# GpSimd waits for the end of short VectorE chains: 42 semaphore waits in an unchanged order (attention with mixture of experts, one Trainium2 core)

## The chip, the cores and the metric

The kernel runs on one core of one Trainium2 chip. The metric is the device time of one launch in microseconds (us), a median over runs. The engines are named as the profile names them: PE is TensorE (PEld its weight loads), DVE is VectorE, ACT is ScalarE, POOL is GpSimd, and SP is SyncE, whose queue issues the DMAs.

## What is computed

Attention over pooled keys, and a top-1 mixture of experts on its output, here cut to the lines that matter:

```
# q [4, 12288, 128], kv [4, 384, 32, 128], w_sr [128, 128]; 8 experts, w1 [8,128,1024], w2 [8,1024,128]
kv_pool = kv.reshape(4, 96, 4, 8, 4, 128).mean(axis=(2, 4))      # 768 keys for each batch
k = v = kv_pool.reshape(4, 768, 128) @ w_sr
a = softmax(q @ k.T / sqrt(128))
x = (a @ v).reshape(49152, 128)
logits = x @ w_gate
e = argmax(logits); gate = softmax(logits)[e]                     # for each token
out = gate * (relu(x @ w1[e]) @ w2[e])
```

## The kernel before

The tokens go through in 96 blocks of 512 (24 for each of the four batches). For a block, PE makes the scores of 768 keys in three pairs of 128 x 512 tiles (`s`), ACT takes the exponential of a pair (`e`, line 974), DVE turns scores and exponentials into the weights `r` (line 976), and PE multiplies them with the values (`po`). A pair of scores keeps its place in PSUM until DVE has written `r`, and there are two such places. ACT, DVE and POOL copy the result and split it into two half-precision parts (`xp`, lines 1010 to 1016), a transposing DMA turns it (`x`), and later PE, ACT and POOL do the expert: hidden units (`b<-x,w1U`), the rectifier on ACT (`g`, and `X` for the first third, which POOL splits in lines 1047 and 1049), the way back on PE (`b<-w2U,g`), DVE's multiplication with the gate (`y`, line 1080) and the store. POOL also splits each block of queries (`qp`, lines 955 and 957) and adds up rows of `kv` for the next batch's keys (lines 443 to 455).

Between the blocks stand pieces that occur once for a batch. `keys` makes the 768 keys and their units; `expert` guesses the batch's commonest expert, loads its weights and sorts its hidden units; `marks` and `count_steps` (lines 1420 to 1424) count the tokens for which the guess does not hold; `general_step` (lines 1213 to 1418) does up to 128 of these in full, once after each of the first three batches. In these pieces DVE has chains of short instructions on tiles of 1 to 384 columns, each needing the one ahead of it: `relative` (lines 584 to 588: five instructions on 128 x 8), `count_steps` (four on 128 x 64), `find` and `find2` (seven and ten, lines 1240 to 1258, nearly all on 128 x 1), and others.

What sets the order: every piece of work is an `op` of a `Plan`, with its engine, a planned duration, a planned time and what it needs. `Plan.order` builds a timetable from these and from hand-set shifts (`NUDGE`), and `Plan.issue` writes the instructions out in that order, so that each engine's instruction stream is fixed. An engine runs its stream in order and waits, by semaphores, for the data and buffers that an instruction needs. `lock=True` keeps an op from being planned at the same time as any POOL op or other locked op; it is a rule of the timetable alone, and nothing holds the engines to it when the program runs. At the start of the program PE also multiplies a constant tile (`slots`) as filler, a fixed number of times.

```
o.lock, o.at0 = lock or eng == "POOL", at        # line 133
if o.lock: start = max(start, locked)            # lines 173, 174
```

Of the kernel before, what the change touches and what calls it, by code (L numbers as in the profile page):

```python
# [18 lines left out]
POOL = 4  # L19
# [92 lines left out]
class Op:  # L112
    pass


class Plan:


    all_ways = False
    LAT = {"PE": 0.28, "ACT": 0.14, "DVE": 0.12, "POOL": 0.14, "SP": 0.1}  # L120

    def __init__(self, slots):
        self.ops, self.slots, self.filler, self.filler_start, self.filler_end = [], slots, None, 0.0, 0.0

    def op(self, eng, us, fn, at, needs=(), gives=(), bufs=(), lands=0.0, moves=0.0, lock=False, way=None):


        if way and WAYS.get(way[0], 0) != way[1] and not self.all_ways:
            return
        o = Op()  # L130
        o.way = way
        o.eng, o.us, o.fn, o.at, o.needs, o.gives, o.bufs, o.lands, o.moves = eng, us, fn, at, needs, gives, bufs, lands, moves
        o.lock, o.at0 = lock or eng == "POOL", at
        o.at = at + sum(NUDGE.get(k, 0.0) for k in self.keys(o))
        o.n = len(self.ops)
        for b in bufs:
            b.left += 1
        self.ops.append(o)
# [89 lines left out]

    def issue(self):
        for o in self.order():  # L230
            for b, first in o.slot_of:
                if first:
                    b.tile = b.make(f"{b.pool}{b.slot}")
            o.fn()


@with_exitstack
def attention_moe(ctx: ExitStack, tc, q, kv, w_sr, w_gate, w1, w2, out):
# [23 lines left out]
    for b in range(B):  # L262
        t = b * NB
# [43 lines left out]
    left, steps, steps_i = keep("left", [P, NL]), keep("steps", [P, NL]), keep("steps_i", [P, NL], I32)  # L307
# [7 lines left out]
    own = keep("own", [P, UH + OWN])  # L315
# [51 lines left out]
    PSUM = {"s": 2, "po": 1, "b": 2}  # L367
    plan = Plan({**SBUF, **PSUM})
    op = plan.op

# [4 lines left out]
    def bank():  # L375
        return buf("b", [P, 512])
# [26 lines left out]
    def keys(b, when):  # L403
# [6 lines left out]
        for d in range(NK // D):  # L410
            at, follow = when(d)
# [9 lines left out]
            if b == 0:  # L421
                pt = pair()
                for i in range(0, POOL, 2):
# [6 lines left out]
                    def add(raw=raw, i=i, pt=pt):  # L430
# [5 lines left out]
                       lock=True)  # L436
# [41 lines left out]
        dg = buf("u", [P, P], BF16)  # L478
# [22 lines left out]
        op("DVE", .3, mean, at - 1, [("vTd", b, d) for d in range(KT // 2)], [("mean", b)])  # L501
        op("DVE", .75, unit_own, at, [("mom", b)], [("own", b)], [dg], lock=True)
        op("PE", .1, lambda: mm(pd.tile[:, :P], ones_b, dg.tile, True, True), at + 1, [("own", b)], [("pd", b)],
# [5 lines left out]
        for n, (lo, hi, w) in enumerate(cuts):  # L509
# [53 lines left out]
    def expert(b, at):  # L563
# [6 lines left out]
        cg = buf("cg", [P, 4, E])  # L570
# [61 lines left out]
        sg = buf("sg", [P, 12, NF])  # L632
# [5 lines left out]
        pz, pu = bank(), bank()  # L638
# [39 lines left out]

        op("DVE", .8, near, at + 11.5, [("u2", b), ("mir", b)], [("key", b)], [pu, sg], lock=True)

# [23 lines left out]
        op("DVE", .17, lambda: chosen(0), at + 15, [("less", b, 0)], [("some0", b)], [la, sg])  # L704
        op("DVE", .35, largest, at + 16, [("less", b, 1), ("some0", b)], [("some", b)], [la, sg])
        pb = bank()
# [6 lines left out]
        cl = buf("cl", [P, NC + 1, NF], BF16)  # L713
# [9 lines left out]

        op("DVE", 1.35, classes, at + 18, [("pb", b)], [("class", b)], [la, pb, cl, sg], lock=True)
        pn = bank()
# [32 lines left out]
        ws = buf("ws", [P, 32])  # L758
# [31 lines left out]
        w2e, w2l = buf("w2e", [P, NF, P + 2], F16), buf("w2l", [P, NF, P], F16)  # L790
# [29 lines left out]

        op("DVE", .4, bias, at + 20, [("ws", b)], [("zp", b)], [w2e, sg], lock=True)

# [78 lines left out]

        op("DVE", .35, biases, at + 30, [("pW", b)], [("zb", b)], [pW, zb])
# [17 lines left out]
        op("DVE", .5, constant, at + 26, [("pown", b), ("uy", b)], [("own2", b)], [po_, ow, ws])  # L920
        op("DVE", .6, constant2, at + 31, [("own2", b), ("w2Ug", b), ("w2x", b)], [("w2U", b)], [ow, w2U], lock=True)
        op("DVE", .1, lambda: nc.vector.memset(cn[:, 31:32], 0.0), at + 36,
# [8 lines left out]
    START, LEN = 42.0, 6.8  # L931
# [281 lines left out]
    def general_step(n=None, at=0.0, follow=()):  # L1213
# [3 lines left out]

        def part(eng, us, fn, needs, gives, bufs=(), lands=0.0):
            if n is None:
                for b in bufs:  # L1220
                    if b.tile is None:
                        i = used[b.pool] = used.get(b.pool, -1) + 1
                        b.tile = b.make(f"{b.pool}{i % plan.slots[b.pool]}")
                fn()
            else:
                here = lambda x: ("general", n, x)
                op(eng, us, fn, at + len(used) * 1.6, [*map(here, needs), *(follow if not needs else ())], [here(gives)], bufs,
                   lands)
                used[len(used)] = 0
# [29 lines left out]

        part("DVE", 1.6, find, [], "find", [gs, gi, le])  # L1260
        vT = buf("gk", [P, NK])
# [9 lines left out]

        part("SP", 3.2, load, ["find"], "load", [gi, vT, *raw], 4.5)
        part("DVE", 1.6, find2, ["find"], "find2", [gs, gi, le])


        NT = NJ + 4
        gp = buf("gp", [P, 2 * NT + 2 * P + 4 + C])
# [13 lines left out]

        part("DVE", 2.0, search, ["find2"], "search", [gs, gp])
        pb = tiny([P, 512])
# [9 lines left out]

        part("DVE", 1.5, select, ["pb"], "select", [gs, gp, pb])
        pr = tiny([P, 512])
# [42 lines left out]
        def top():  # L1348
# [6 lines left out]
                                                      bias=nmax(), scale=scale, accum_out=sums()), ["top"], "a", [gs, ps, a])  # L1355
# [36 lines left out]

        part("DVE", .7, weight, ["ex"], "w", [gs])

# [12 lines left out]
        py, o = tiny([P, 512]), buf("pool", [P, C])  # L1407
# [34 lines left out]
    for t in range(NBLK):  # L1442
        block(t)
        if t == NBLK - LAST:
            marks(B - 1, START + (t + 3) * LEN, (B - 1) * NB, t, False)
        if t % NB == NB - 1:
            b = t // NB
            if b < B - 1:
                marks(b, START + (t + 4) * LEN, b * NB, t + 1, True)
            else:  # L1450
                marks(b, START + (t + 3) * LEN, t + 1 - LAST, t + 1, True)
            op("DVE", 1.8, count_steps, START + (t + 5) * LEN + 3, [("left", b)], [("steps", b)])
            if b in STEPS_AFTER:
                general_step(b, START + (t + 10) * LEN, [("steps", b), ("stored", b)] + [("o", i) for i in range(b * NB, t + 1)])
# [39 lines left out]
```

## Time and profile before

| | us |
|---|---|
| median of 3 runs | 817.34 (816.2 to 818.12) |
| profiled execution | 819.5 |
| its span, from the first to the last instruction | 817.7 |

| engine | busy us | share of the span |
|---|---|---|
| PE | 759.8 | 93% |
| DVE | 652.2 | 80% |
| POOL | 601.1 | 74% |
| ACT | 592.2 | 72% |

The chain of work that ended last lies 62% on PE, 18% on DVE, 7% in DMAs, 6% on POOL and 3% on ACT. PE had its full clock in nearly all of the span. To read it: the shares are averages over 96 nearly equal blocks and a few places that differ from them, so the stretches are looked at one by one.

### The profile page before, as it was taken

Reading aid. Unit: us, or ns where it says so; the run is one execution under the profiler, and the core shown is the slowest. Engines: PE = TensorE matmul, PEld = TensorE weight load, DVE = VectorE, ACT = ScalarE, POOL = GpSimd, SP = SyncE. Lnnn points to the kernel's source line nnn. Section 1 sums busy time; section 2 is a strip of 40 time slices with the busy share of each in tenths; the row PEclk is TensorE's granted clock in tenths of the full one; section 3 lists DMA queues with packets and bytes.
Section 4 is the critical chain, followed back from the end, with each engine's and each line's share of the span. In section 5 each row is a group of like instructions: output and inputs, shape, how many; then the busy total and the mean of one; then the engine's idle time right before and its main releaser. Section 6 shows DMA issues by size and latency. Waiting matters only on the chain.

```text
span 817.7 us, 21949 instructions
## 1 busy us (share of the span) xinstructions
PE 759.8 (93%) x8535; PEld 597.3 (73%) x8535; DVE 652.2 (80%) x1224; ACT 592.2 (72%) x949; POOL 601.1 (74%) x802
## 2 busy tenths in 40 slices
PE   5978999999998988999998978999999999999996
PEld 4547777788786766788776756787787777787875
DVE  5767876888877988878979888788896899868684
ACT  1435878778788766877878767888878878788773
POOL 0543599976779978996778788987767888566545
PEclk9989999999999999999999999999999999999999
DMA  9642999894589987897659789979467789757543
GB/s 338 207 99 53 185 210 256 185 208 103 111 212 173 240 201 190 201 172 169 118 138 218 161 208 222 233 166 202 109 127 153 162 165 226 147 116 136 126 84 93
DMA packets 328282, 139.45 MB, mean 171 GB/s; under 512 B 214590, under 2 KB 320194, under 8 KB 328176
## 3 DMA queue, kind: packets, MB, share of 16 engines
q1 hardware_dynamic: 327696, 137.80, 76.4%
q8 instruction: 67, 1.10, 0.6%
q14 instruction: 39, 0.32, 0.1%
q0 software_dynamic: 192, 0.17, 0.1%
q10 hardware_dynamic: 288, 0.07, 0.0%
HBM read 59.12 MB, written 26.94 MB: 105 GB/s over the span
## 4 chain that ended last, share of the span: by engine, by line
PE 62%; DVE 18%; DMA 7%; POOL 6%; issue 3%; ACT 3%; SPq 0%; DVEq 0%; POOLq 0%; ACTq 0%
PE b L353 30%; PE po L353 17%; PE s L353 13%; DVE r L976 8%; DMA qT<-qp 4%; DMA kv<-in_kv_dram 2%; POOL kv L443 2%; DVE y L1080 1%; ACT e L974 1%; DVE junk L1181 1%; DVE xp L1011 1%; POOL g L1049 1%; DMA x<-xp 1%; DVE la L698 1%; DVE PU L746 0%
## 5 line engine op out<-in xcount | busy, mean ns | idle before, releaser
L976 DVE SCALAR_TENSOR_TENSOR r<-s,e 128x1024 bf16<-128x1024 f32 x288 | 346.2, 1215 | 66.5 <-ACT e L974 64.7
L974 ACT ACTIVATE e<-s 128x1024 f32<-128x1024 f32 x288 | 292.5, 1026 | 95.8 <-PE s L353 88.1
L353 PE MATMUL po<-v,r 128*128 128x145 f16 x2304 | 253.7, 228 | 6.7 <-DVE xp L1011 3.2
L353 PE MATMUL s<-qT,KT 128*128 128x512 f16 x576 | 170.5, 384 | 20.1 <-DVE r L976 12.7
L353 PEld LDWEIGHTS <-r 128*128 128x128 bf16 x2304 | 169.1, 99 | 26.9 <-DVE xp L1011 3.8
L353 PE MATMUL b<-w2U,g 128*128 128x128 f16 x1736 | 159.8, 219 | 1.0 <-POOL g L1049 1.0
L353 PE MATMUL b<-x,w1U 128*128 128x512 f16 x465 | 141.9, 381 | 4.2 <-ACT g L1053 1.4
L353 PE MATMUL po<-M,qT 128*128 128x136 f16 x1152 | 131.8, 224 | 0.0
L353 PE MATMUL b<-L,x 128*128 128x128 f16 x1116 | 123.0, 219 | 0.6 <-ACT pT L467 0.3
L1053 ACT ACTIVATE g<-b,zb 128x512 f16<-128x512 f32 x146 | 99.4, 689 | 25.8 <-PE b L353 24.9
L1049 POOL TENSOR_TENSOR g<-X,g 128x512 f16<-128x512 f32 x96 | 112.8, 1175 | 6.5
L957 POOL TENSOR_TENSOR qp<-qr,qp 128x512 f16<-128x512 f32 x94 | 110.4, 1175 | 5.3
L353 PEld LDWEIGHTS <-g 128*128 128x128 f16 x1736 | 113.0, 98 | 1.2 <-POOL g L1049 1.1
L353 PEld LDWEIGHTS <-qT 128*128 128x128 f16 x1152 | 85.4, 98 | 32.2 <-issue 6.9
L353 PEld LDWEIGHTS <-x 128*128 128x128 f16 x1116 | 81.0, 98 | 17.8 <-issue 2.8
L1047 POOL CAST g<-X 128x512 f16<-128x512 f32 x96 | 60.8, 634 | 41.5 <-ACT X L1045 37.5
L353 PEld LDWEIGHTS <-KT 128*128 128x128 bf16 x576 | 51.2, 100 | 53.4 <-issue 23.2
L955 POOL CAST qp<-qr 128x512 f16<-128x512 f32 x94 | 59.1, 630 | 36.7 <-DMA qr<-in_q_dram 25.2
L1080 DVE TENSOR_TENSOR y<-b,gt 128x512 f32<-128x512 f32 x96 | 65.3, 681 | 17.8 <-PE b L353 12.7
L1045 ACT ACTIVATE X<-b,zb 128x512 f32<-128x512 f32 x96 | 66.4, 693 | 16.8 <-PE b L353 16.1
L353 PEld LDWEIGHTS <-w1U 128*128 128x128 f16 x480 | 45.6, 99 | 35.5 <-issue 4.3
L443 POOL TENSOR_TENSOR kv<-kv,kv 128x1024 f32<-128x1024 f32 x27 | 63.6, 2356 | 6.3 <-DMA kv<-in_kv_dram 5.4
(365 smaller groups left out, 992.3 us busy)
## 6 DMA issues: line engine op xcount, KB each, us to landing
qr<-in_q_dram SPq DMA_DIRECT2D x96, 256.0 KB, 3.4
out_dram<-y SPq DMA_DIRECT2D x96, 256.0 KB, 2.8
kv<-in_kv_dram SPq DMA_DIRECT2D x41, 512.0 KB, 6.5
raw<-in_moe_w_dram SPq DMA_DIRECT2D x14, 512.0 KB, 5.5
e<-in_kv_dram SPq DMA_DIRECT2D x3, 512.0 KB, 8.6
v_dram<-vT SPq DMA_DIRECT2D x4, 384.0 KB, 2.9
qT<-qp SPq DMA_TRANSPOSE x94, 3.4
x<-xp SPq DMA_TRANSPOSE x93, 3.5
```

Source lines behind the costliest of these rows:

```text
L353: return nc.tensor.matmul(o, l, r, start=start, stop=stop)
L443: nc.gpsimd.tensor_add(flat(to), flat(to), flat(of))
L698: nc.vector.tensor_scalar(lc(2 + NC * j, NC), limits, lc(j), key(j), op0=ALU.is_ge, op1=ALU.mult)
L955: op("POOL", .62, lambda: nc.gpsimd.tensor_copy(qp.tile[:, 0], qr.tile), T - 1.9 * LEN, [("qr", t)], [("qh", t)], [qr, qp])
L957: op("POOL", 1.17, lambda: nc.gpsimd.tensor_sub(qp.tile[:, 1], qr.tile, qp.tile[:, 0]), T - 1.8 * LEN, [("qh", t)], [("qp", t)], [qr, qp])
L974: op("ACT", 1.03, lambda e=e, ps=ps: nc.scalar.activation(e.tile, ps.tile, AF.Exp), at + .6, [("s", t, s)], [("e", t, s)], [ps, e])
L976: op("DVE", 1.22, lambda e=e, ps=ps, s=s: nc.vector.scalar_tensor_tensor(r.tile[:, 2 * s:2 * s + 2], ps.tile, 1.0, e.tile, op0=ALU.add, op ...
L1045: op("ACT", .69, lambda ph=ph, zu=zu: nc.scalar.activation(gf.tile, ph.tile, AF.Relu, bias=zu()), at + .5, [("ph", t, u), ("zb", b)], [("g ...
L1047: op("POOL", .62, lambda: nc.gpsimd.tensor_copy(gg.tile[:, 0], gf.tile), at + 1.5, [("gf", t)], [("gh", t), ("g", t)], [gf, gg])
L1049: op("POOL", 1.16, lambda: nc.gpsimd.tensor_sub(gg.tile[:, UH], gf.tile, gg.tile[:, 0]), at + 2, [("gf", t), ("gh", t)], [("g", t)], [gf, gg])
L1053: op("ACT", .69, lambda u=u, ph=ph, zu=zu: nc.scalar.activation(gg.tile[:, u], ph.tile, AF.Relu, bias=zu()), at + .5, [("ph", t, u), ("zb" ...
L1080: op("DVE", .69, lambda: nc.vector.tensor_tensor(y.tile, py.tile.rearrange("p (c d) -> p c d", d=C), bc(gr["gt"].tile[:, 0, js], C), op=AL ...
```

## The change

POOL's stream and all others keep their order. Fourteen kinds of DVE op get the mark `whole=True`. When such an op has been written out, the next POOL op in the order, if the timetable starts it within 2.5 us after the marked op's planned end, gets a semaphore wait on the marked op's last instruction. There are 42 such places, each wait on one instruction, and one POOL op at most for each marked op. In 19 of them POOL's instruction already had a wait, and a separate waiting instruction stands ahead of it.

```diff
 class Op:
-    pass
+    whole = False
 class Plan:
+    FOLLOW = 2.5
-        o.lock, o.at0 = lock or eng == "POOL", at
+        o.lock, o.at0, o.whole = lock or eng == "POOL", at, whole
     def issue(self):
+        block, last = self.tc.nc.cur_bb.bb, None
         for o in self.order():
             for b, first in o.slot_of:
                 if first:
                     b.tile = b.make(f"{b.pool}{b.slot}")
+            n = len(block.instructions)
             o.fn()
+            if o.whole:
+                last = o, block.instructions[-1]
+            if o.eng == "POOL" and last and o.start < last[0].start + last[0].us + self.FOLLOW:
+                first = next(i for i in block.instructions[n:] if i.engine == mybir.EngineType.Pool)
+                self.tc.add_manual_dep(first, last[1].name, mybir.DependencyInfo(
+                    mybir.DependencyClass.Sync, mybir.DependencyReason.DATA), reason="order")
+                last = None
...
-        op("DVE", 1.0, relative, at + 2, [("first", b)], [("cg", b)], [cg], lock=True)
+        op("DVE", 1.0, relative, at + 2, [("first", b)], [("cg", b)], [cg], lock=True, whole=True)
...
-            op("DVE", 1.8, count_steps, START + (t + 5) * LEN + 3, [("left", b)], [("steps", b)])
+            op("DVE", 1.8, count_steps, START + (t + 5) * LEN + 3, [("left", b)], [("steps", b)], whole=True)
```

The other twelve marks are set in the same way: in `keys` on `unit_own`; in `expert` on `near`, `largest`, `classes`, `bias`, `biases` and `constant2`; in `general_step` on `find`, `find2`, `search`, `select` and `weight`.

## Rows read from the trace of the kernel before

**Rows 1.** The page, part 1: busy time, share of the span and instructions by engine.
```profile
PE 759.8 (93%) x8535; PEld 597.3 (73%) x8535; DVE 652.2 (80%) x1224; ACT 592.2 (72%) x949; POOL 601.1 (74%) x802
```
**Rows 2.** Waits of PE: who waited for whom, us in total, times, longest.
```profile
PE s L353 <- DVE r L976: 12.7, 19, 5.7
```
**Rows 3.** Timeline, 38.9 to 58: start, us, instruction, [idle before, releaser].
```profile
38.96 4.78 POOL L443 TENSOR_TENSOR kv<-kv,kv 128x1024 f32<-128x1024 f32 x2
39.57 1.76 DVE L584 TENSOR_SCALAR cg<-iota_e,con 128x8 f32<-128x8 f32 x1
...
41.57 2.19 DVE L586 TENSOR_TENSOR cg<-cg,wg_raw 128x8 f32<-128x8 f32 x1
...
43.87 2.33 POOL L443 TENSOR_TENSOR kv<-kv,kv 128x1024 f32<-128x1024 f32 x1
43.99 2.24 DVE L588 TENSOR_SCALAR cg<-wg_raw,cg 128x8 f32<-128x8 f32 x1
...
47.41 0.59 PE L353 MATMUL s<-qT,KT 128*128 128x512 f16 x1 [5.65 <-DVE r L976]
...
57.60 0.20 POOL L665 TENSOR_TENSOR sg<-sg 128x8 f32<-128x8 f32 x1 [9.25 <-DVE sg L658]
```
**Rows 4.** Lines 584, 586, 588: ns minimum/median/maximum, first and last start us.
```profile
L584 DVE TENSOR_SCALAR cg<-iota_e,con x4: 218/460/1764, 39.6 to 562.0; 128x8 f32<-128x8 f32 x4
...
L586 DVE TENSOR_TENSOR cg<-cg,wg_raw x4: 166/589/2195, 41.6 to 562.9; 128x8 f32<-128x8 f32 x4
...
L588 DVE TENSOR_SCALAR cg<-wg_raw,cg x4: 231/526/2239, 44.0 to 563.3; 128x8 f32<-128x8 f32 x4
```
**Rows 5.** Stretches: us, PE, PEld, DVE, ACT, POOL busy (count), PE clock, DMA share, GB/s.
```profile
47.40:53.20 5.80, 5.79 (x17) 2.54 (x17) 3.54 (x3) 2.05 (x2) 0.87 (x2) 0.50 0.27 68
...
292.10:295.50 3.40, 3.40 (x12) 1.24 (x10) 3.19 (x19) 1.81 (x3) 0.40 (x2) 0.50 0.28 80
...
479.80:483.20 3.40, 3.40 (x28) 2.85 (x26) 1.88 (x3) 1.37 (x3) 2.36 (x4) 0.50 0.67 157
```
**Rows 6.** Timeline, 286 to 292: the first `count_steps` on DVE, and PE behind it.
```profile
286.47 2.23 DVE L1422 TENSOR_SCALAR steps_i<-steps_i 128x64 int32<-128x64 int32 x1
...
288.74 1.31 DVE L1423 CAST steps<-steps_i 128x64 f32<-128x64 int32 x1
...
291.87 0.30 PE L353 MATMUL po<-v,r 128*128 128x145 f16 x2 [1.97 <-DVE r L976]
```
**Rows 7.** Lines 1422 to 1424: ns minimum/median/maximum over the four batches.
```profile
L1422 DVE TENSOR_SCALAR steps_i<-steps_i x4: 195/615/2230, 286.5 to 812.8; 128x64 int32<-128x64 int32 x4
...
L1423 DVE CAST steps<-steps_i x4: 195/618/1309, 288.7 to 813.1; 128x64 f32<-128x64 int32 x4
...
L1424 DVE TENSOR_TENSOR_SCAN ends<-steps x4: 291/678/2359, 290.1 to 813.3; 128x64 f32<-128x64 f32 x4
```
**Rows 8.** Timeline, 474 to 481: the second `count_steps`, PE and POOL behind it.
```profile
474.70 1.04 DVE L1423 CAST steps<-steps_i 128x64 f32<-128x64 int32 x1
...
475.77 2.36 DVE L1424 TENSOR_TENSOR_SCAN ends<-steps 128x64 f32<-128x64 f32 x1
...
478.76 0.22 PE L353 MATMUL po<-v,r 128*128 128x145 f16 x1 [2.89 <-DVE xp L1011]
...
480.68 0.22 POOL L1114 TENSOR_TENSOR gt<-gt 128x16 f32<-128x16 f32 x1 [2.70 <-DVE gt L1111]
```
**Rows 9.** Timeline, 489 to 499: `find2` on DVE, `g` on POOL, its first reader on PE.
```profile
489.42 0.61 POOL L1047 CAST g<-X 128x512 f16<-128x512 f32 x1
...
491.52 0.45 DVE L1255 TENSOR_TENSOR gs<-gs 128x1 f32<-128x1 f32 x1
...
492.25 0.27 DVE L1258 TENSOR_TENSOR step<-step,gs 128x1 f32<-128x1 f32 x1
...
495.67 1.69 POOL L1049 TENSOR_TENSOR g<-X,g 128x512 f16<-128x512 f32 x1
...
498.89 0.39 PE L353 MATMUL b<-w2U,g 128*128 128x128 f16 x4
```

More of the change, by code (lines that the diff above doesn't have):

```diff
@@ L123, in __init__, with op @@
         self.ops, self.slots, self.filler, self.filler_start, self.filler_end = [], slots, None, 0.0, 0.0
-    def op(self, eng, us, fn, at, needs=(), gives=(), bufs=(), lands=0.0, moves=0.0, lock=False, way=None):
+    def op(self, eng, us, fn, at, needs=(), gives=(), bufs=(), lands=0.0, moves=0.0, lock=False, way=None,
+           whole=False):
         if way and WAYS.get(way[0], 0) != way[1] and not self.all_ways:
@@ L368, in attention_moe @@
     plan = Plan({**SBUF, **PSUM})
+    plan.tc = tc
     op = plan.op
@@ L501, in keys @@
         op("DVE", .3, mean, at - 1, [("vTd", b, d) for d in range(KT // 2)], [("mean", b)])
-        op("DVE", .75, unit_own, at, [("mom", b)], [("own", b)], [dg], lock=True)
+        op("DVE", .75, unit_own, at, [("mom", b)], [("own", b)], [dg], lock=True, whole=True)
         op("PE", .1, lambda: mm(pd.tile[:, :P], ones_b, dg.tile, True, True), at + 1, [("own", b)], [("pd", b)],
@@ L677, in near @@
                                            op1=ALU.bitwise_or)
-        op("DVE", .8, near, at + 11.5, [("u2", b), ("mir", b)], [("key", b)], [pu, sg], lock=True)
+        op("DVE", .8, near, at + 11.5, [("u2", b), ("mir", b)], [("key", b)], [pu, sg], lock=True, whole=True)
         def spread():
@@ L704, in expert @@
         op("DVE", .17, lambda: chosen(0), at + 15, [("less", b, 0)], [("some0", b)], [la, sg])
-        op("DVE", .35, largest, at + 16, [("less", b, 1), ("some0", b)], [("some", b)], [la, sg])
+        op("DVE", .35, largest, at + 16, [("less", b, 1), ("some0", b)], [("some", b)], [la, sg], whole=True)
         pb = bank()
@@ L722, in classes @@
             nc.vector.scalar_tensor_tensor(c[:, 2], col(7), top(2), c[:, NC], op0=ALU.is_lt, op1=ALU.subtract)
-        op("DVE", 1.35, classes, at + 18, [("pb", b)], [("class", b)], [la, pb, cl, sg], lock=True)
+        op("DVE", 1.35, classes, at + 18, [("pb", b)], [("class", b)], [la, pb, cl, sg], lock=True, whole=True)
         pn = bank()
@@ L819, in bias @@
             nc.vector.tensor_tensor(z[:, :, P + 1], col(5), z[:, :, P], op=ALU.subtract)
-        op("DVE", .4, bias, at + 20, [("ws", b)], [("zp", b)], [w2e, sg], lock=True)
+        op("DVE", .4, bias, at + 20, [("ws", b)], [("zp", b)], [w2e, sg], lock=True, whole=True)
         pL = bank()
@@ L900, in biases @@
             nc.vector.scalar_tensor_tensor(zb.tile, zb.tile, 1.0 / Z_DOWN, own[:, :UH], op0=ALU.mult, op1=ALU.add)
-        op("DVE", .35, biases, at + 30, [("pW", b)], [("zb", b)], [pW, zb])
+        op("DVE", .35, biases, at + 30, [("pW", b)], [("zb", b)], [pW, zb], whole=True)
         op("ACT", .7, lambda: nc.scalar.activation(w2U.tile[:, :UH], wide()[:, :, :P],
@@ L920, in expert @@
         op("DVE", .5, constant, at + 26, [("pown", b), ("uy", b)], [("own2", b)], [po_, ow, ws])
-        op("DVE", .6, constant2, at + 31, [("own2", b), ("w2Ug", b), ("w2x", b)], [("w2U", b)], [ow, w2U], lock=True)
+        op("DVE", .6, constant2, at + 31, [("own2", b), ("w2Ug", b), ("w2x", b)], [("w2U", b)], [ow, w2U], lock=True, whole=True)
         op("DVE", .1, lambda: nc.vector.memset(cn[:, 31:32], 0.0), at + 36,
@@ L1216, in general_step, with part @@
         used = {}
-        def part(eng, us, fn, needs, gives, bufs=(), lands=0.0):
+        def part(eng, us, fn, needs, gives, bufs=(), lands=0.0, whole=False):
             if n is None:
@@ L1227, in part @@
                 op(eng, us, fn, at + len(used) * 1.6, [*map(here, needs), *(follow if not needs else ())], [here(gives)], bufs,
-                   lands)
+                   lands, whole=whole)
                 used[len(used)] = 0
@@ L1258, in find2 @@
             nc.vector.tensor_tensor(step, step, u(7), op=ALU.add)
-        part("DVE", 1.6, find, [], "find", [gs, gi, le])
+        part("DVE", 1.6, find, [], "find", [gs, gi, le], whole=True)
         vT = buf("gk", [P, NK])
@@ L1272, in general_step @@
         part("SP", 3.2, load, ["find"], "load", [gi, vT, *raw], 4.5)
-        part("DVE", 1.6, find2, ["find"], "find2", [gs, gi, le])
+        part("DVE", 1.6, find2, ["find"], "find2", [gs, gi, le], whole=True)
         NT = NJ + 4
@@ L1290, in search @@
             nc.vector.memset(q_sb(), 0.0)
-        part("DVE", 2.0, search, ["find2"], "search", [gs, gp])
+        part("DVE", 2.0, search, ["find2"], "search", [gs, gp], whole=True)
         pb = tiny([P, 512])
@@ L1302, in select @@
             nc.vector.tensor_tensor(sel0(), sel(), sel0(), op=ALU.subtract)
-        part("DVE", 1.5, select, ["pb"], "select", [gs, gp, pb])
+        part("DVE", 1.5, select, ["pb"], "select", [gs, gp, pb], whole=True)
         pr = tiny([P, 512])
@@ L1391, in weight @@
             nc.vector.tensor_tensor(z(3), z(0), z(2), op=ALU.mult)
-        part("DVE", .7, weight, ["ex"], "w", [gs])
+        part("DVE", .7, weight, ["ex"], "w", [gs], whole=True)
         h = buf("gp", [P, NF, TAIL])
```

## The prediction

> **What bounds the kernel now.** First the busy table of the page: PE is busy for 759.8 of 817.7 us, DVE for 652.2, POOL for 601.1 [rows 1]. So PE sets the time, and an edit that touches only DVE and POOL can win no more than PE's idle time and what PE loses at half clock. Next the waits of PE: it stands 12.7 us before the scores `s`, waiting for DVE's `r`; one of the 19 waits is 5.7 us long [rows 2]. The timeline shows what DVE does in that wait: three instructions on 128 x 8 take 1.76, 2.19 and 2.24 us [rows 3], while the same lines take 0.22, 0.17 and 0.23 at best [rows 4]. Their ends are those of POOL's additions of `kv`: POOL's pair runs from 38.96 to 43.74 and DVE's second long one ends at 43.76; POOL's third runs from 43.87 to 46.20 and DVE's third ends at 46.23 [rows 3]. The short instruction is held until POOL's long one is over, and `r`, queued behind it on DVE, is held too. The same is seen in `count_steps` at 286 [rows 6] and at 474 [rows 8]. Last the PE clock: after each of these three waits PE stays at 0.50, the lower of its two levels (1.2 GHz instead of 2.4), and is busy all the time [rows 5].
>
> **The change, part by part.** No instruction moves and nothing is added on DVE, PE, ACT or SP. On POOL 42 instructions wait for the end of a DVE chain, so that a chain which has not met a POOL instruction yet meets none. The gain is the stretching of the chain; the price is that POOL, and everything queued behind its waiting instruction, starts later. Of the added waiting instructions the trace of before shows nothing that I can price apart; they stand in POOL's idle time before the wait ends, and I count them at zero (bounds: none, and the 1.0 us of the last term).
>
> *The start (38.9 to 53).* Stretching: (1.76 - 0.22) + (2.19 - 0.17) + (2.24 - 0.23) = 5.57 us [rows 3, 4]. The waiting POOL instruction is the very one at 38.96, so the chain, which begins at 39.57, runs clean and ends near 40.66; `r` comes 5.6 us earlier and of PE's 5.65 us some 0.1 is left: -5.5. POOL begins 1.7 us later, and the 9.25 us in which it sits idle before 57.60 [rows 3] hide that; without this cover the 1.7 us would fall on the first `mirror` and on PE behind it. With the idle time goes the cause of the half clock that stands right behind it: 5.79 us of PE work at 0.50 would take 2.9 us at full clock [rows 5]. That is -2.9 if PE alone sets the pace and 0 if the clock falls all the same; I take -2.2, three quarters, because DVE and ACT work for 3.54 and 2.05 us of the stretch and stand between the pairs of scores. Together **-7.7** (ends -5.5 and -8.4).
>
> *The first `count_steps` (286 to 295.5).* Stretching of its second and third instruction: (2.23 - 0.20) + (1.31 - 0.20) = 3.1 us [rows 6, 7]. PE idles 1.97 us for the `r` behind them [rows 6] and then works 3.40 us at half clock, which is 1.7 us more than at full [rows 5]; PE could win 3.7, DVE gives 3.1. I take **-3.0** (ends -2.0 and -3.7). POOL's `kv` addition starts some 1.0 us later.
>
> *The second (474 to 499).* Stretching: (1.04 - 0.20) + (2.36 - 0.29) = 2.9 us [rows 7, 8]. PE idles 2.89 us [rows 8] and loses another 1.7 at half clock [rows 5]: 4.6 at most. Here POOL is next. Its queue starts again at 480.68, after an idle time of 2.70 us [rows 8]; the additions ahead of it move 1.1 us back by the wait, so it can start at 479.1 at best, 1.5 us earlier. At 495.67 + 1.69 = 497.36 POOL ends a `g` that PE reads first at 498.89, which is a cover of 1.5 us [rows 9]. So PE can come 1.5 + 1.5 = 3.0 us earlier before it waits for that `g`, and only 1.5 where a DMA behind POOL's work decides. I take **-2.2**, the middle of 1.5 and 2.9 (ends 0 and -4.6).
>
> *The other places.* The remaining 18 waits for `r` sum to 7.0 us [rows 2]. Where PE is busy throughout, a shorter chain wins nothing. I count a fifth, **-1.5**, for waits right behind one of the other 39 chains (ends 0 and -3).
>
> *What the waits cost.* At 489.42 POOL starts a `g` that will wait for `find2`, which ends at 492.25 + 0.27 = 492.52 [rows 9]: up to 3.1 us later, with POOL's queue behind it (that `g`, the pooled keys, `xp`, `qp`, the next `g`, and SP's transposing DMAs for them). Against the cover of 1.5 us that is 1.0 to 1.6 us on PE if POOL has no work left over. Most places have longer covers, so I count this once: **+1.0** (ends 0 and +4).
>
> A rule that speaks against part of this. Of `find2`'s ten instructions, on 128 x 1, only the two with two tiles as inputs were long, 0.45 and 0.27 us; they hold 0.7 us together, so the wait wins less than that and costs POOL up to 3.1 [rows 9]. The Trainium skill (SBUF — State Buffer, "Who interferes with whom") says that a VectorE instruction with at most one SBUF input contends with GpSimd only in a two-port mode. By that the waits for `find2` buy next to nothing, as the row has it; if no one-input instruction were ever held, the start would win 2.0 us (its one `TENSOR_TENSOR`) and not 5.6. The rows of lines 584 and 588, with one tile and one scalar column, show 1.76 and 2.24 us, so I keep the sum by the rows; it counts nothing for `find2`.
>
> **The sum.** -7.7 - 3.0 - 2.2 - 1.5 + 1.0 = -13.4 us. The profiled execution took 819.5 us (span 817.7 and 1.8 around it), so its like would take 806.1. The median of the runs is 817.34, 2.2 lower; from it 803.9.
>
> **The rivals.** (a) *The start alone.* What DVE gives back at 286 and 474 is lost again, because PE then waits for POOL, which starts later and has no idle time there. For it: POOL's 1.5 us against DVE's 2.9. Against it: at 286 the chain is the only thing that PE waits for. Time: 817.3 - 7.7 + 1.0 = 810.6, and 812 without part of the clock.
> (b) *Slower.* POOL's idle time reaches PE through `g`. Place: the places where a `g` stands in POOL's queue within some 3 us of a waiting instruction, as at 489.42 [rows 9]. Price: the wait less the cover, 3.1 - 1.5 = 1.6 us, and, once PE stands for some 2 us as at 290, 1.7 us of half clock behind it: 3.3 each. It decides from the fifth such place on (13.4 + 1.0 against 5 x 3.3); at six the time is 817.3 - 14.4 + 19.8 = 822.7. Against it: POOL works 601 of 818 us [rows 1], and most `g` that I looked at are ready 2 us or more before PE reads them.
> (c) *It does not do what it says.* The wait holds only POOL instructions behind it in the queue; one that already runs still blocks the chain. If the long additions were already under way in the three large places, nothing would change: 817.3, within 0.2%. Against it: at 38.96 it is the waiting instruction itself that blocks.
> (d) *More.* PE takes the full 8.4, 3.7 and 4.6 and POOL is hidden: 817.3 - 16.7 - 3.0 = 797.6.
>
> **How the numbers follow.** Forecast (799 to 808): 0.62; (a) 0.22; (d) 0.05; (c) 0.05; (b) 0.06. The likeliest gives 803.9. The range reaches to (a) and to the edge of (d): 798 to 812, leaving out (b), (c) and part of (d). About 0.2%, or 1.6 us, is what a measurement of this kernel can tell from no change. Faster: 0.62 + 0.22 + 0.05 = 0.89; within 0.2%: 0.05; slower: 0.06.
>
> **What would show it.** Right, if lines 584 to 588 at 39.6 take 0.16 to 0.23 us each, PE's 5.65 us before `s` is gone, the PE clock stays at 1.00 from 41 to 54, and `s` of 47.41 starts near 41.9; if lines 1422 to 1424 take 0.2 to 0.3 us and the half clock behind 292 and 480 is gone; if POOL's idle time put down to DVE grows while PE's idle time put down to `g` of POOL stays under some 3 us. Wrong, if the chains stay long (c), if new waits of PE for `g`, or for DMAs behind `xp` and `qp`, stand behind the waiting places, with new stretches at 0.50 (b), or if everything after 60 us keeps its old length (a).

## The result, and the profile after

The changed kernel takes 808.89 us (median, 805.28 to 813.16), against 817.6 for the kernel before in the same measurement: a ratio of 0.9884, with an interval of 0.9845 to 0.9922. That is faster by 1.2%, 5 us above the predicted time and inside its range. The quotient of the two medians is 0.9893 (8.7 us); the gains below are worked out from the ratios of interleaved runs, by which this kernel gains 1.16% of 817.6 us, 9.5 us. In the listing of after, line numbers are 14 or 15 higher: 584 to 588 are now 599 to 603, and 1422 to 1424 are 1437 to 1439.

First the page of after, busy time by engine. Against [rows 1], PE, ACT and POOL have their old work, and DVE has lost 24 us:
```profile
PE 758.4 (94%) x8535; PEld 600.7 (74%) x8535; DVE 628.3 (78%) x1224; ACT 591.5 (73%) x949; POOL 599.2 (74%) x802
```
DVE executes the same 1224 instructions. The 24 us were never work; nearly all of them were time for which short instructions were held. The chains of `relative` and `count_steps` are now clean in all four batches. After, by line: ns minimum/median/maximum, first and last start (compare [rows 4] and [rows 7]):
```profile
L599 DVE TENSOR_SCALAR cg<-iota_e,con x4: 221/222/223, 43.5 to 554.0; 128x8 f32<-128x8 f32 x4
...
L603 DVE TENSOR_SCALAR cg<-wg_raw,cg x4: 231/231/231, 44.4 to 554.9; 128x8 f32<-128x8 f32 x4
...
L1437 DVE TENSOR_SCALAR steps_i<-steps_i x4: 195/195/195, 280.0 to 803.6; 128x64 int32<-128x64 int32 x4
...
L1439 DVE TENSOR_TENSOR_SCAN ends<-steps x4: 291/291/291, 280.4 to 804.0; 128x64 f32<-128x64 f32 x4
```
Not every marked chain came clean. In `general_step` a POOL instruction that already runs when the chain begins, or that an earlier wait has just let go, still holds it:
```profile
474.10 1.17 POOL L972 TENSOR_TENSOR qp<-qr,qp 128x512 f16<-128x512 f32 x1
474.24 1.11 DVE L1256 TENSOR_TENSOR le<-le,ends 128x64 f32<-128x64 f32 x1
```
This is `find` at its second place in after; the same instruction took 0.55 us there in before. POOL's next addition waited for `find`, began at 476.12, and held `find2`'s line 1270 to 0.66 us (0.45 in before).

The start in the timeline of after (start, us, instruction, [idle before, releaser]; compare [rows 3]):
```profile
42.51 0.59 PE L367 MATMUL s<-qT,KT 128*128 128x512 f16 x2 [0.38 <-DVE r L991]
...
43.50 0.22 DVE L599 TENSOR_SCALAR cg<-iota_e,con 128x8 f32<-128x8 f32 x1
...
44.36 0.23 DVE L603 TENSOR_SCALAR cg<-wg_raw,cg 128x8 f32<-128x8 f32 x1
...
44.67 4.78 POOL L458 TENSOR_TENSOR kv<-kv,kv 128x1024 f32<-128x1024 f32 x2 [1.74 <-DVE cg L603]
```
The chain runs first, in 1.1 us, and POOL's addition waits 1.74 us for it. PE's longest wait for `r` in this stretch falls from 5.65 to 0.38 us.

Then the waits of PE in after (waiting engine, tile and line, releaser: us in total, times, longest; compare [rows 2]):
```profile
PE b L1352 <- DMA gp<-in_q_dram,gi: 6.3, 2, 4.0
PE s L367 <- DVE r L991: 5.8, 13, 1.2
...
PE b L367 <- POOL g L1064: 1.1, 2, 0.7
```
The last of these lines read so in before:
```profile
PE b L353 <- POOL g L1049: 1.0, 1, 1.0
```
`r` has fallen from 12.7 to 5.8 us, and the waits for `g`, with which the prediction was concerned, sum to 1.1 us, against 1.0 in before: next to nothing has come of a late `g`. The first line is new: in the trace of before PE never waits for this DMA. It is the gather in `general_step`, an indirect DMA (line 1333, 1318 before) that fetches the rows of queries numbered in `gi`. POOL issues it, from its own queue.

The second of these waits, in the timeline of after:
```profile
492.01 1.16 POOL L972 TENSOR_TENSOR qp<-qr,qp 128x512 f16<-128x512 f32 x1 [1.28 <-DVE gp L1317]
...
496.98 0.15 DVE L1330 CAST gi<-gs 128x1 int32<-128x1 f32 x1
...
498.28 1.91 SPq L433 DMA_DIRECT2D kv<-in_kv_dram  x3
...
498.50 0.61 POOL L970 CAST qp<-qr 128x512 f16<-128x512 f32 x1
...
499.26 1.12 POOL L1333 DMA_INDIRECT gp<-in_q_dram,gi  x1 [0.16 <-issue]
...
506.21 0.45 PE L1352 MATMUL b<-ident,gp 128*128 128x128 f32 x1 [4.00 <-DMA gp<-in_q_dram,gi]
```
and the same place in the timeline of before:
```profile
511.57 0.15 DVE L1315 CAST gi<-gs 128x1 int32<-128x1 f32 x1
...
512.36 1.12 POOL L1318 DMA_INDIRECT gp<-in_q_dram,gi  x1 [0.16 <-issue]
...
512.74 2.79 SPq L418 DMA_DIRECT2D kv<-in_kv_dram  x3
...
516.52 0.28 PE L1337 MATMUL b<-ident,gp 128*128 128x128 f32 x1
```
Two things differ. POOL comes to the gather 2.1 us after the row numbers are there (499.26 less 497.13) instead of 0.6: it stood 1.28 us for the end of `select` (line 1317) and worked without a pause from there to the gather. And the first of SP's three loads of `kv`, 0.5 MB each, now stands 1.0 us ahead of the gather and the last 0.3 us behind it; in before the first stood 0.4 us behind. From issue to first use the gather takes 6.95 us, against at most 4.16 before. (The third gather, near 700 us, is issued 0.3 us after its row numbers and nothing waits for it, in all kernels here.)

The clock of after in five stretches (us; PE, PEld, DVE, ACT, POOL busy and count; granted clock, DMA share, GB/s; compare [rows 5]):
```profile
41.90:45.90 4.00, 3.49 (x19) 1.65 (x18) 3.86 (x9) 2.06 (x2) 2.26 (x2) 1.00 1.24 275
61.90:65.30 3.40, 3.40 (x18) 3.40 (x17) 3.19 (x8) 1.23 (x3) 0.00 (x0) 0.50 0.00 0
283.20:286.60 3.40, 3.37 (x35) 2.24 (x32) 3.19 (x17) 3.10 (x5) 2.40 (x3) 1.00 0.32 87
...
481.70:485.10 3.40, 3.39 (x30) 3.09 (x29) 1.80 (x6) 1.19 (x3) 3.32 (x4) 0.50 1.11 309
...
505.70:509.00 3.30, 2.79 (x10) 1.96 (x11) 0.39 (x1) 1.46 (x3) 3.22 (x3) 0.50 1.16 280
```
At the start and behind the first `count_steps` the clock stays at 1.00. Behind the 4 us for the gather it is 0.50, the lower of its two levels (1.2 of 2.4 GHz), which makes this place dearer than its wait. The stretch at 482 us stands behind the second `count_steps`, where before had one at 479.8 [rows 5]: it moved, and did not go. The stretch at 62 us is new; PE's nearest wait is one of 0.83 us at 59.8, which before has too.

### The profile page after: what moved, and what is told of

It reads as the page before. It is cut to its first block, busy times and chain, and to the rows that moved or that the text cites. A ratio compares the mean times of both kernels' runs of the same rounds, so it can differ in the third digit from the quotient of the medians.

```text
span 808.5 us, 21968 instructions
## 1 busy us (share of the span) xinstructions
PE 758.4 (94%) x8535; PEld 600.7 (74%) x8535; DVE 628.3 (78%) x1224; ACT 591.5 (73%) x949; POOL 599.2 (74%) x802
## 4 chain that ended last, share of the span: by engine, by line
PE 63%; DVE 12%; POOL 9%; DMA 8%; ACT 4%; issue 3%; SPq 0%; POOLq 0%; DVEq 0%; ACTq 0%
PE b L367 31%; PE po L367 17%; PE s L367 14%; DVE r L991 5%; DMA qT<-qp 3%; POOL kv L458 3%; DMA kv<-in_kv_dram 2%; ACT e L989 2%; DMA gp<-in_q_dram,gi 1%; POOL g L1064 1%; DVE y L1095 1%; POOL qp L972 1%; POOL g L1062 1%; DMA x<-xp 1%; ACT g L1068 1%
## 5 line engine op out<-in xcount | busy, mean ns | idle before, releaser
L367 PEld LDWEIGHTS <-r 128*128 128x128 bf16 x2304 | 167.6, 98 | 24.8 <-DVE xp L1026 4.0
L367 PE MATMUL s<-qT,KT 128*128 128x512 f16 x576 | 168.4, 380 | 9.4 <-DVE r L991 5.8
L367 PE MATMUL b<-w2U,g 128*128 128x128 f16 x1736 | 161.6, 220 | 1.4 <-POOL g L1064 1.1
L1062 POOL CAST g<-X 128x512 f16<-128x512 f32 x96 | 58.7, 612 | 39.0 <-ACT X L1060 29.2
L367 PEld LDWEIGHTS <-KT 128*128 128x128 bf16 x576 | 50.7, 99 | 40.2 <-issue 13.4
```

Source lines behind the costliest of these rows:

```text
L367: return nc.tensor.matmul(o, l, r, start=start, stop=stop)
L1062: op("POOL", .62, lambda: nc.gpsimd.tensor_copy(gg.tile[:, 0], gf.tile), at + 1.5, [("gf", t)], [("gh", t), ("g", t)], [gf, gg])
```

## Where the time went, stage by stage

PE executes the same instructions in the same order in every kernel here, so the time between the starts of two of its instructions can be compared between traces. This table is worked out so from the timelines. The stages by their time in before are: the start (41.1 to 53.3), the first `count_steps` (280.1 to 300.0), the first gather (321.1 to 330.0), the second `count_steps` (474.0 to 493.0), what follows (493.0 to 516.0), and the second gather (516.0 to 530.0). The kernels below the first two belong to the experiments; "others" are the waits in `keys` and `expert` but for `relative` of the first batch.

| kernel | start | count 1 | gather 1 | count 2 | behind | gather 2 |
|---|---|---|---|---|---|---|
| before | 12.1 | 19.9 | 9.0 | 19.0 | 23.1 | 14.0 |
| after (all 42 waits) | 4.0 | 16.9 | 11.5 | 14.7 | 24.1 | 19.5 |
| start alone | 4.0 | 19.0 | 9.0 | 19.0 | 22.8 | 15.3 |
| `count_steps` alone | 10.7 | 16.3 | 11.5 | 14.7 | 25.3 | 14.1 |
| others alone | 11.0 | 19.9 | 9.0 | 19.0 | 25.5 | 14.2 |
| `general_step` alone | 10.7 | 18.3 | 13.1 | 19.1 | 22.9 | 19.7 |
| all but `general_step` | 4.0 | 16.3 | 13.0 | 14.7 | 24.8 | 14.1 |
| all but `select` | 4.0 | 16.9 | 13.1 | 14.7 | 25.8 | 14.1 |
| all, gather earlier | 4.0 | 17.0 | 9.6 | 14.7 | 24.1 | 15.9 |

From before to after the start gives 8.1 us, the two `count_steps` 3.0 and 4.3. The stage behind the second takes 1.0 back, the gathers 2.5 and 5.5. Between the first `count_steps` and the first gather (300.0 to 321.1, not in the table) another 2.1 us are won, 1.3 with the waits of `count_steps` alone, so a part of what the first gather takes had been won just ahead of it.

## The experiments

The first theory (A) was that the waits of `general_step` make POOL late for its own gather, and that this, and not a late `g`, is what the change lost. The rival (B) was that the loss lies elsewhere: in POOL being late in general, or in the clock. A second question was which marks carry the gain. All ratios are to the kernel before, from runs interleaved with it; the interval is in brackets.

**All marks but the five in `general_step`.**
```diff
-        part("DVE", 1.6, find, [], "find", [gs, gi, le], whole=True)
+        part("DVE", 1.6, find, [], "find", [gs, gi, le])
...
-        part("DVE", .7, weight, ["ex"], "w", [gs], whole=True)
+        part("DVE", .7, weight, ["ex"], "w", [gs])
```


> The marks of the five chains of general_step (find, find2, search, select, weight) are taken off; the other nine kinds keep theirs. Theory A (the waits of general_step make POOL late for its own indirect DMA, the gather of the query rows, on which PE then stands 2.3 us at 312 and 4.0 us at 506): both waits of PE for the gather are under 0.5 us, the gains at the start and at the two count_steps stay, and the time is 6 to 9 us below the changed kernel, 800 to 803 us, ratio to before 0.979 to 0.983. Theory B (the 8 us are lost elsewhere, by POOL being late in general or by the half clock at other places): the time stays at 807 to 810 us, ratio 0.988 to 0.991.

0.9826 [0.9797, 0.9854], 4.7 us below the changed kernel; the intervals just overlap. The second gather stage fell from 19.5 to 14.1 us, with no wait for the gather and no half clock, as theory A has it. The first did not fall: 13.0 us, part of it a stretch at the low clock. There PE still stands 2.13 us:
```profile
308.40 1.29 POOL L1333 DMA_INDIRECT gp<-in_q_dram,gi  x1 [0.17 <-issue]
...
314.69 0.30 PE L1352 MATMUL b<-ident,gp 128*128 128x128 f32 x1 [2.13 <-DVE r L991]
```
The row names `r`, but by the profile the gather landed 0.13 us before this instruction, as in the kernels whose rows name the gather. So theory A's forecast of under 0.5 us at both places failed at the first. POOL issues the gather 1.6 us after the row numbers, though no wait of `general_step` is left. So this stall has a second cause.

**All marks but `select`.**
```diff
-        part("DVE", 1.5, select, ["pb"], "select", [gs, gp, pb], whole=True)
+        part("DVE", 1.5, select, ["pb"], "select", [gs, gp, pb])
```


> Only the mark of select (the last chain ahead of the gather of query rows) is taken off. Theory A (the gather is late because POOL's queue ahead of it waits for select): half of the loss is won back or more, PE waits under 2 us for the gather at each of its places, 804 to 806 us, ratio 0.983 to 0.987. Theory A2 (the delay builds up over find, find2 and search, select adds nothing): 807 to 809 us, PE's waits for the gather stay at 2 to 4 us. Theory B (the gather is not the cause): no change either, and PE's idle time moves to another place.

0.9840 [0.9816, 0.9864]. The second stage is 14.1 us again, the first 13.1 with a wait of 2.3, where theory A had under 2. At the second place, then, taking off the wait on the last chain ahead of the gather is enough to undo the loss.

**All 42 waits, the gather earlier in POOL's stream.** This takes away the lateness and leaves the waits.
In the diff `("general", 0, "q")` is the gather of the first batch, `("qh", 37)` the first half of the split of block 37's queries, and `("gh", 52)` that of block 52's `g`; `at` finds an op's index in the order.
```diff
+    AHEAD = [(("general", 0, "q"), ("qh", 37)), (("general", 1, "q"), ("gh", 52))]
+    def early(self, ops):
+        at = lambda g: next(i for i, o in enumerate(ops) if o.eng == "POOL" and tuple(o.gives)[:1] == (g,))
+        for q, other in self.AHEAD:
+            o = ops.pop(at(q))
+            ops.insert(at(other), o)
+        return ops
...
-        for o in self.order():
+        for o in self.early(self.order()):
```


> The changed kernel with all of its 42 waits; only the gather moves ahead in POOL's stream: at its first place ahead of one split of queries (qp, 1.8 us of POOL), at its second ahead of one split of g and the copy of a qp (2.4 us). Theory A (POOL, which runs late behind the waits, issues the gather 2 to 3 us after its row numbers are there, and PE stands for it): POOL issues it 1.5 to 2.5 us sooner against its neighbours on PE, PE's two waits fall from 2.3 and 4.0 us to under 0.6 and under 2, the half clock behind the second goes, and the time is 3 to 7 us below the changed kernel: 802 to 806 us, ratio to before 0.981 to 0.986. Theory B (the gather is slow in itself, or the row numbers come late): no change, 807 to 810 us, ratio 0.988 to 0.991.

0.9818 [0.9779, 0.9857], 5.4 us below the changed kernel. POOL issues the gathers 1.2 and 0.3 us after their row numbers instead of 3.0 and 2.1, and the waits of PE are 0.44 and 1.12 us instead of 2.33 and 4.00. The wait for the gather in this kernel (its listing is another 9 lines longer, so that the gather is line 1342):
```profile
PE b L1361 <- DMA gp<-in_q_dram,gi: 1.6, 2, 1.1
```
No wait was removed; only the gather's place in POOL's queue changed. The two gather stages are 1.9 and 3.6 us shorter, together as much as the time, and with the two runs before it that decides for A against B, though the intervals of this kernel and the changed one just touch. At the second place 1.8 of the 2.9 us by which the wait fell are the earlier issue; the rest is the gather itself, which took 1.0 us less from issue to first use.

**The waits of `general_step` alone.** The marks of the other nine kinds are off, the five in `general_step` stay.

> Only the waits of the five chains in general_step, on an otherwise unchanged kernel. Theory A (the waits cost by themselves, since POOL is late for the gather whatever PE does): PE stands 2 to 4 us for the gather twice, 2 to 6 us slower than before, ratio 1.002 to 1.008. Theory C (they cost only where PE comes earlier than before, by the gains at other places): within 1.5 us of before, ratio 0.998 to 1.002.

1.0062 [1.0030, 1.0094]: 5.1 us slower than before. PE waits for the gather at the same two places and for as long as in the changed kernel:
```profile
PE b L1352 <- DMA gp<-in_q_dram,gi: 6.1, 2, 3.9
```
The price is the same as beside the gains at other places (+6.2 and +5.8 thousandths), as far as the intervals can tell. (The stage of the first gather is 13.1 us here because 3.4 us of half clock follow the wait of 2.24.)

**One wait alone: `relative` of the first batch.**
```diff
-        op("DVE", 1.0, relative, at + 2, [("first", b)], [("cg", b)], [cg], lock=True, whole=True)
+        op("DVE", 1.0, relative, at + 2, [("first", b)], [("cg", b)], [cg], lock=True, whole=b == 0)
```
(and no other mark)

> One wait alone is kept of the 42: POOL's addition of kv at 38.96 waits for relative of the first batch. Theory A (the stretching at the start is 5.5 us of PE's idle time and the half clock behind it): -7 to -9 us, 808 to 810 us, ratio 0.989 to 0.991, lines 584 to 588 at 39.6 take 0.16 to 0.25 us, and everything behind 60 us keeps its length. Rival (what the start gives is taken back by a later stage, because POOL or ACT sets the pace there): ratio 0.995 to 1.0.

0.9943 [0.9913, 0.9974], 4.6 us: between the two forecasts, and neither's. The stage fell from 12.1 to 4.0 us, as in every kernel with this wait. In the timed runs less arrives than in the trace of the stage, a point taken up below.

**The four waits of `count_steps` alone**, all else unmarked.

> Only the four waits for count_steps. The traces so far give, by stage: 3.0 to 3.6 us less from 280 to 300, 4.3 us less from 474 to 493, and given back 2.4 us at the first gather and some 2 us from 493 to 516. Theory E (what DVE gains here meets POOL's and the gather's own pace): 2 to 4 us below before, ratio 0.995 to 0.998, PE waits 2 us for the gather at its first place. The prediction's terms (3.0 and 2.2 us, nothing lost at the gather): 5.2 us, ratio 0.9925 to 0.9945.

0.9959 [0.9925, 0.9992], 3.4 us. The stages gave 3.6 and 4.3 us, gave back 2.2 behind the second, and 2.5 at the first gather, where PE waits 2.33 us, as theory E has it. This is the second cause: DVE has the row numbers some 3 us sooner and PE comes 3 us sooner, but POOL's queue ahead of the gather is as long as before. In before POOL stood waiting for the row numbers there:
```profile
315.70 0.15 DVE L1315 CAST gi<-gs 128x1 int32<-128x1 f32 x1
...
316.16 1.29 POOL L1318 DMA_INDIRECT gp<-in_q_dram,gi  x1 [0.64 <-DVE gi L1315]
```
Now the row numbers wait for POOL, 1.6 us.

**The first `relative` and `count_steps` together**, five waits.

> Five waits of the 42 are kept: relative of the first batch and count_steps of the four batches. Theory A (three places carry the gain): start -8, first count_steps -3.5, second -2 to -4, no wait for the gather: 801 to 804 us, ratio 0.980 to 0.984. Rival (the gain at count_steps is taken back by POOL's later g, and the other waits hold a good part of the gain): 807 to 810 us, ratio 0.988 to 0.991.

0.9884 [0.9852, 0.9915], 9.5 us. The time is the rival's. Of the 7.9 us that the two `count_steps` stages give, 1.7 are taken back behind the second and 2.4 at the first gather, where PE waits 2.26 us; theory A had no such wait.

**All but `general_step`, the first gather earlier.** The version of the first experiment, with the gather of the first batch ahead of one split of queries on POOL.
```diff
+    AHEAD = [(("general", 0, "q"), ("qh", 37))]
```


> The version without the waits of general_step, and in it the gather of the first batch stands ahead of one split of queries on POOL. There PE stood 2.1 us at 314.7, with the half clock behind it. Theory A (what the first count_steps gave is taken back there because POOL gets to the gather 1.6 us after its row numbers): PE's wait is under 0.6 us, and the time is 2 to 4 us below the version without it, 800 to 802 us, ratio 0.978 to 0.981. Rival (the split that is pushed back delays the transposed queries, and PE waits for these instead): no gain, ratio 0.982 to 0.985, with a new wait of PE for qT.

0.9786 [0.9742, 0.9830], median 801.65 us: the fastest kernel here. The first gather stage is 9.0 us, as in before; POOL now waits for the row numbers, and PE for nothing:
```profile
302.52 1.29 POOL L1342 DMA_INDIRECT gp<-in_q_dram,gi  x1 [0.65 <-DVE gi L1339]
...
307.84 0.27 PE L1361 MATMUL b<-ident,gp 128*128 128x128 f32 x1
```
The stage is 4.0 us shorter than without the move; the intervals of the two kernels overlap. In this trace the stage behind the second `count_steps` is 28.9 us, 4 longer than without the move, with 6.8 us at the low clock.

**The same move with five waits** (`relative` of the first batch and `count_steps`).

> The version with five waits (relative of the first batch, four count_steps), and in it the gather of the first batch ahead of one split of queries on POOL. Without that move it had a ratio of 0.9884, and PE stood 2.3 us for that gather. If the many other waits carry nothing that lasts: as fast as the version with them and the same move (ratio 0.9786), 0.977 to 0.982. If they carry 4 to 5 us: 0.983 to 0.987, and then the two stages from 75 to 252 us are 2 us or more longer than in the version with all of them.

0.9888 [0.9848, 0.9928]. The stage is 9.0 us here too, but the time is that of the five waits without the move, so this pair does not show the 2.4 us of the stage. It lies outside both forecasts. Against the version before it, it is 8 us slower by the ratios and 5.5 by the medians. The many small chains carry something, then; from 75 to 252 us the kernel that has them is 1.6 us shorter, not the 2 or more of the forecast.

**The others alone** (`keys` and `expert`, without the first `relative`).

> The waits of keys and expert alone: none at relative of the first batch, none at count_steps, none in general_step. The prediction put 1.5 us on all such places together; the difference between the runs with five waits and without those of general_step is 4 to 5 us. Theory D (many small chains sum to 4 to 5 us): ratio 0.993 to 0.996. Theory of the prediction (1 to 2 us): 0.997 to 1.0. A third outcome, 0.999 or above, would say that they win only where the start and count_steps are mended too.

1.0006 [0.9974, 1.0038], the third outcome. In the trace of this kernel the low clock stands at 18, 46, 66 and 76 us; before has only the second of these. The last three:
```profile
45.70:52.50 6.80, 3.59 (x11) 1.55 (x11) 5.51 (x4) 1.75 (x2) 3.99 (x3) 0.51 0.52 116
66.10:69.50 3.40, 3.40 (x18) 3.40 (x18) 2.63 (x8) 1.54 (x2) 0.28 (x1) 0.51 0.00 0
76.10:79.50 3.40, 3.40 (x31) 2.85 (x29) 1.59 (x11) 0.63 (x1) 1.76 (x2) 0.52 0.41 77
```
To see whether these waits need a mended start or a mended `count_steps` beside them, the two missing combinations were run.

> The waits of keys and expert with that of the first relative, without count_steps and general_step. Alone the start has a ratio of 0.9943 and the others 1.0006; with count_steps all three have 0.9826, while the start and count_steps without the others have 0.9884. Theory F (the others carry 4 to 6 us, and lost it in their own run to the half clock about the unmended start): 0.986 to 0.990. Theory G (they carry nothing, and the difference of the pairs is scatter): 0.993 to 0.996.

0.9867 [0.9821, 0.9913].

> The same without the wait of the first relative, and with the four of count_steps (alone 0.9959). Theory F (the others need the mended start): 0.994 to 0.998, as count_steps alone. Theory H (the others carry 4 to 6 us whatever stands beside them, and their own run was scatter): 0.988 to 0.991.

0.9892 [0.9839, 0.9945]. Theory F holds for the first of the two, theory H for the second: the others add 5 to 6 us beside either of them. It is their run alone that stands out.

The traces show where these waits win. PE takes 45.0 to 45.1 us for its instructions from 170 to 215 us in all six traces without them and 43.7 to 43.8 in all eight with them; from 560 to 605 it takes 44.9 to 45.0 and 43.7; from 395 to 425, 29.9 and 29.8. That is 2.7 us together, whatever stands beside them, their own run included. One of the waits of before that they remove:
```profile
200.70 0.59 PE L353 MATMUL s<-qT,KT 128*128 128x512 f16 x2 [0.60 <-DVE r L976]
```
So their own run did not lack the gain. Its trace lost it elsewhere: at the low clock shown above, and behind the second `count_steps`, where the two kernels that have these waits and not those of `count_steps` take 25.5 and 25.7 us instead of 23.1. Whether that alone makes the 1.0006 is not shown.

With these, all eight combinations of three groups of waits have been timed, and what a group does is the mean of four differences (each ratio's interval is some 0.003 to 0.005 wide to either side, so a mean is good to about 2 us; the third number of the first two rows and the first of the third rest on the run that stands out):

| group | the four differences of ratios, in thousandths | mean, us |
|---|---|---|
| first `relative` | -5.7, -7.5, -13.9, -6.6 | -6.9 |
| `count_steps` | -4.1, -5.9, -11.4, -4.1 | -5.2 |
| others | +0.6, -6.7, -7.6, -5.8 | -4.0 |
| `general_step` (two differences) | +6.2, +5.8 | +4.9 |

## Why the prediction was right, and where it was off

*What bounds the kernel, and how the chains come clean*: right. DVE and POOL do not share the time; a short instruction is held to the end of POOL's long one. Lines 599 and 603 take 0.22 and 0.23 us at every start once POOL's addition waits. Rival (c), that a POOL instruction already under way still blocks the chain, came true in `general_step`: line 1256 of `find` takes 0.55 to 1.34 us in after, 0.23 to 0.55 in before.

*The start, -7.7*: right in size. The stage fell by 8.1 us in the trace; the timed combinations give 6.9. The half clock behind the wait went too, and was worth 2.6 us (8.1 less 5.5) where 2.2 had been taken. A part of it came back: in most traces with this wait 3.4 to 6.8 us at the low clock stand somewhere from 56 to 73 us, and make the stage from 58 to 75 us 0.6 to 3.3 us longer than the 17.0 of before. Since three kernels without this wait have 18.6 to 19.3 there too (`count_steps`, `general_step` and the others, each alone), this looks like scatter from one execution to the next more than a consequence.

*The two `count_steps`, -3.0 and -2.2*: right in size, in part by luck. The first stage gave 3.0 in after. The second gave 4.3, and some of it was lost behind it: 1.0 in after and 2.2 with these waits alone, so 2.1 to 3.3 in the end. But the loss is not at the `g` that the step named. PE waits 1.2 to 1.6 us there for the `r` that DVE writes behind `find2` (0.26 in before), and `find` and `find2` are held by POOL's instructions, as shown above; in after PE's idle time in this stage did not grow (2.5 us, 2.8 in before), and the 3.4 us at the low clock from 481.7 are what makes it longer. Nor had the step the 2.4 us at the first gather. So the 5.2 us of the table equal the predicted 5.2 by terms that offset each other, and its four differences reach from 3.4 to 9.3.

*The other places, -1.5*: too small; the combinations give -4.0. The term counted a fifth of PE's waits for `r`. But a clean chain also frees DVE for all that stands behind it: DVE is busy for 24 us less in after, and the chains that PE waits for directly are only some of these. By the traces 2.7 us of them arrive from 170 to 215, 395 to 425 and 560 to 605 us, in every kernel with these waits; the rest is within what the mean can tell.

*What the waits cost, +1.0 at one `g`*: this is the step that failed. The runs put it at +4.9. The second gather's stage grew by 5.5 us; the 2.5 us at the first arise with the waits of `count_steps` alone, too, and cannot be put down to those of `general_step` by themselves. The place was `general_step`, as predicted, and the cause was POOL's queue behind its waits (at the second place that of `select` alone undoes it), but the tile was another. The step listed what was queued behind the waiting `g`: pooled keys, `xp`, `qp`, the next `g`, SP's transposing DMAs. It stopped before the gather, which stands in the same queue 23 us behind that `g` (489.42 to 512.36 in before), and whose result PE had read without a wait. A DMA that POOL issues has no engine in the table of waits until it is late; in the trace of before its cover could have been read: the two gathers landed 4.4 and 3.7 us after their issue, and PE read them first after 5.3 and 4.2, a cover of 0.9 and 0.5 us. At the named `g` PE waits 0.80 us in three traces (`general_step` alone, all but `select`, all with the gather earlier) and not at all in after.

*The rule that spoke against part of the change*: the Trainium skill (SBUF — State Buffer, "Who interferes with whom") lets a one-input instruction be held only in a two-port mode, and counts the tensor-with-scalar form among those that can enter one. By that rule the five instructions of `relative` could win anything from 2.0 us to all of it. The trace agrees with the long end: lines 599 and 603, one tile and one scalar column, fell from 1.76 and 2.24 us to 0.22 and 0.23 when nothing but POOL's start was moved. The waits of `find2` were not tested by themselves. At the second place they bought nothing in after, where `find2`'s two instructions with two tiles take 0.66 and 0.16 us (0.45 and 0.27 in before); with those of the four other chains of `general_step` they lose 4.9 us.

*The sum.* By groups it would have been -6.9 - 5.2 - 4.0 + 4.9 = -11.2 us, where -13.4 were predicted and -9.5 (1.16% of 817.6) measured. Two terms were wrong by 2.5 and 3.9 us with opposite signs, so that the sum came as near as it did is in part luck. The groups do not simply add up either: the first three are -16.1 us by the table and -14.2 when they stand together. The prediction also took 0.2% for what a measurement of this kernel can tell; the interval of the result is 0.4% to either side, 3.1 us and so as large as either term for `count_steps`. Of the rivals, (b) named the right kind of mechanism with the wrong tile, and at a price that two places could not raise to what the other terms gave.

## What to carry to other kernels

A wait that keeps a slow engine out of another's way is paid by everything in the slow engine's queue, and the DMAs that this engine issues are part of that queue: follow it to its next DMA, and compare the issue with the first use. Put such waits where the protected chain holds up the bound engine and no such DMA is near: here the marks outside `general_step` won 14 us together, and the five in it cost 5. If a wait must stay, move the DMA ahead of the work that the wait holds back, which won 5.4 us here without removing a wait. And look at what a held POOL instruction runs into when it is let go: in `general_step` that was the next short chain.

## What the runs showed of the hardware

The gather's time varies, and goes with the loads that SP issues beside it. At its second place it took 6.9 us from issue to first use, with PE waiting, in the two kernels where the first of three loads of `kv` was issued 0.9 to 1.0 us ahead of it (the changed kernel, and the waits of `general_step` alone); in before, 4.16 and without a wait. So a lateness that grew by 1.5 us became a wait of 4.0. From issue to landing, over all 14 traces: at the third place, with no load of `kv` within 9 us, 3.3 to 3.5 us; at the first, 3.6 to 4.9 with the loads 3.6 us behind the gather, 4.4 to 4.7 with 1.7 us, 5.0 to 6.4 with 0.3 to 0.4; at the second, 3.7 to 5.8 with the loads 0.4 us or more behind, 6.8 with the first ahead. That the loads are the cause was not tested by moving them alone, and at one distance the times still differ by up to 2 us.

How small an instruction can be and still be held shows in the same traces. One-input instructions on 128 x 1 reading 128 x 1 took at most 0.22 us in all 14. One on 128 x 2 (line 785 in after, at 573.1) took 1.08 us instead of 0.17 and ended with POOL's split.

PE falls to its lower clock also behind short waits, and not each time. From 61.9 to 65.3 in after it is busy for 3.40 of 3.40 us at 0.50, with no DMA traffic at all; ahead of that stands this wait:
```profile
59.80 1.97 PE L367 MATMUL b<-ones,kv 128*128 128x64 f32 x16 [0.83 <-DVE ws L784]
```
Before has the same wait of 0.83 us at 64.05 and keeps 1.00 behind it. The first 41 us of after are 3.8 us longer than those of before, for the most part by such a stretch, and no wait of the change precedes it: the first marked chain starts at 34.06. The kernel with five waits, the first of them later still, has a stretch at 0.50 at the same place. That of after:
```profile
17.50:24.30 6.80, 6.17 (x29) 6.17 (x30) 3.99 (x4) 0.00 (x0) 1.65 (x2) 0.50 0.60 178
```
The runs of after lie 7.9 us apart, with a mean granted clock of 0.985 in the longest (813.16) and 0.995 in the shortest (805.28). That is as much as the largest term of the sum, so differences of a few microseconds had to be read by stages and not from single runs.
